# A searched order for the head of a fused attention and MLP kernel, with the fillers in free columns of a fixed PSUM bank

## The chip, the cores and the metric

The kernel runs on one core of a Trainium2 chip. The time is the device time of one execution in microseconds (us). The span in a profile is 1.7 to 1.8 us shorter than the time of the same execution (576.9 for 578.67 before).

PE is the matrix engine (TensorE), DVE is VectorE, ACT is ScalarE, POOL is GpSimd, SP is SyncE. The **head** is the work on batch 0 up to its MLP, some 45 us; the seven later batches run at full density behind it.

## The reference, cut to what matters

```python
# q, k, v: (8, 12, 448, 64); U (448, 32), V (32, 448); w_ch1 (768, 3072), w_ch2 (3072, 768)
q_n, k_n = rmsnorm(q, g_q), rmsnorm(k, g_k)      # x / sqrt(mean(x*x) + 1e-6) * g
attn = softmax(q_n @ k_n.T / 8)
x = (attn @ v)                                   # heads side by side: (8, 448, 768)
u = x + (x.T @ U @ V).T
out = u + relu(u @ w_ch1) @ w_ch2
```

## The kernel before

Inputs come in tiles of four heads of one batch; batch 0 has tiles 0, 1 and 2. For a tile, POOL or ACT squares q and k, DVE sums the squares (`reduce`), ACT makes the reciprocal root (`rsqrt`), DVE multiplies it in (`scale`), PE transposes (`turn`), and per pair of heads PE makes scores, ACT exponentials, PE weighs the values and DVE normalises. The head is a list of such pieces, and the schedule is by hand: each engine runs its instructions in the order of this list, and waits where an operand isn't ready (in the profile before, POOL stood 7.03 us for a scale of tile 2, with a cast and the issue of w1's third piece behind it in its order).

First, w1 is loaded in four pieces, and POOL issues them:

```python
def load_w1(i):
    c = (slice(0, 512), slice(512, 1024), slice(1024, 2048), slice(2048, 3072))[i]
    nc.gpsimd.dma_start(w1b[:, :, c], w1r[:, :, c])
```

The third piece, `load_w1(2)`, has hidden columns 1024 to 2047: blocks 8 to 15 of the first layer of the MLP need it. Second, a helper that makes POOL wait for a scale of DVE, by copying one element of its result. Third, the squares, which for tiles 2 to 5 are POOL's:

```python
def yield_port(t, pr):
    nc.gpsimd.tensor_copy(scratch, qkns[2 * t + pr][0:1, 1, 0, 0, 0:1])

def squares(t, hs=ALL, ss=(0, 1), eng=None):
    for s in ss:                                   # s = 0: k, s = 1: q
        ...
        if (t < 2 or t > 5) and eng is None:
            nc.scalar.activation(sqs[t, s][:, hs], qks[t, s][:, hs], AF.Square)
        else:
            nc.gpsimd.tensor_tensor(sqs[t, s][:, hs], qks[t, s][:, hs], qks[t, s][:, hs], OP.mult)
```

Fourth, the fillers, matmuls whose results nobody reads, and the list, here around `load_w1(2)`. The fillers are meant to keep PE's clock up:

```python
def heat(n):
    if n:
        warm = ps_mm.tile([P, 512], FP32, tag="mm")
        for _ in range(n):
            nc.tensor.matmul(warm, cold[:, 0:P], cold[:, 0:512], start=True, stop=True)

plan = [
    (heat, 16),
    ...
    (scores, 5, (0,)),
    (weigh, 3, 1),
    (load_w1, 2),
    (spread, 0),
    (squares, 3, ALL, (1,)),
    ...
]
```

## Time and profile before

| | before |
|---|---|
| time, median of 5 executions | 579.18 us (578.57 to 579.65) |
| span of the profiled execution | 576.9 us |
| PE busy | 560.0 us, 97% |
| MLP of batch 0 starts | 45.07 us |
| third piece of w1: issued, landed | 33.48, 50.25 us |
| block 8 starts (first use of that piece) | 50.29 us |

PE is busy nearly all the time, so the time goes with what PE loses, and it loses most in the head. The prediction below shows the page, the PE timeline and the chain of waits. The table of stretches before (stretch and its length, then busy time and count of PE, PE's weight loads, DVE, ACT and POOL, the granted PE clock, the DMA share and GB/s):

```profile
20.00:30.00 10.00, 8.40 (x101) 5.57 (x102) 7.90 (x19) 6.59 (x11) 4.66 (x8) 0.66 1.16 252
30.00:40.00 10.00, 10.00 (x177) 6.95 (x174) 8.49 (x24) 9.52 (x15) 7.62 (x7) 1.00 1.15 256
...
60.00:80.00 20.00, 18.34 (x194) 10.94 (x192) 16.78 (x40) 12.05 (x18) 7.36 (x10) 1.00 1.30 212
```

The clock was 0.66 in the mean from 20 to 30 us: the cold stretch. And the DVE timeline before, at the first scales of tile 2 (start, duration, engine, line, operation, tiles, count, and in brackets the idle time before and what ended it):

```profile
24.38 1.30 DVE L253 TENSOR_TENSOR qkn<-hT,rstd 112x512 bf16<-112x512 f32 x2 [0.19 <-issue]
```

Two scales in 1.30 us.

### The profile page before, as it was taken

Reading aid. Unit: us, or ns where it says so; the run is one execution under the profiler, and the core shown is the slowest. Engines: PE = TensorE matmul, PEld = TensorE weight load, DVE = VectorE, ACT = ScalarE, POOL = GpSimd, SP = SyncE. Lnnn points to the kernel's source line nnn. Section 1 sums busy time; section 2 is a strip of 40 time slices with the busy share of each in tenths; the row PEclk is TensorE's granted clock in tenths of the full one; section 3 lists DMA queues with packets and bytes.
Section 4 is the critical chain, followed back from the end, with each engine's and each line's share of the span. In section 5 each row is a group of like instructions: output and inputs, shape, how many; then the busy total and the mean of one; then the engine's idle time right before and its main releaser. Section 6 shows DMA issues by size and latency. Waiting matters only on the chain.

```text
span 576.9 us, 11306 instructions
## 1 busy us (share of the span) xinstructions
PE 560.0 (97%) x4607; PEld 306.5 (53%) x4607; DVE 387.1 (67%) x755; ACT 281.4 (49%) x419; POOL 79.0 (14%) x124
## 2 busy tenths in 40 slices
PE   5799999999999999999999999999999999999997
PEld 2465556544565555544465555644456555654464
DVE  4885964799875787647776598747767487453442
ACT  4777543376621875166641676246661475302200
POOL 4772510100020000000020000000011000000010
PEclk9799999999999999999999999999999999999999
DMA  9999985544443555544525455555334441050021
GB/s 212 243 252 226 216 139 141 129 118 88 112 136 93 117 135 126 114 99 113 129 75 116 105 130 120 125 132 128 82 79 127 122 97 33 28 110 1 1 55 55
DMA packets 103648, 67.22 MB, mean 117 GB/s; under 512 B 54716, under 2 KB 102060, under 8 KB 103596
## 3 DMA queue, kind: packets, MB, share of 16 engines
q1 hardware_dynamic: 93988, 56.77, 42.0%
q0 software_dynamic: 9376, 9.44, 9.8%
q8 instruction: 36, 0.59, 0.4%
q10 hardware_dynamic: 232, 0.30, 0.2%
q14 instruction: 16, 0.13, 0.1%
HBM read 52.19 MB, written 11.01 MB: 110 GB/s over the span
## 4 chain that ended last, share of the span: by engine, by line
PE 87%; DVE 4%; DMA 4%; ACT 1%; issue 0%; POOL 0%; DVEq 0%; ACTq 0%
PE ph L538 36%; PE pb L463 10%; PE po L463 8%; PE o L323 8%; PE pe L463 7%; PE pa L463 7%; PE sc L297 7%; DMA w1b<-in_moe_w_ch_dram 3%; DVE qkn L253 2%; PE pu L376 2%; ACT E L302 1%; DVE ring L378 1%; DMA u<-ring 1%; PE pm L362 1%; PE pt L264 0%
## 5 line engine op out<-in xcount | busy, mean ns | idle before, releaser
L538 PE MATMUL ph<-u,w1b 128*128 128x512 bf16 (+1 forms) x1128 | 232.6, 354 | 2.7 <-DVE qkT L275 1.2
L302 ACT ACTIVATE E<-sc 112x896 bf16<-112x896 f32 x184 | 159.8, 914 | 61.1 <-PE sc L297 61.0
L538 PEld LDWEIGHTS <-w1b 128*128 128x128 bf16 x1128 | 102.9, 98 | 110.9 <-issue 23.1
L463 PEld LDWEIGHTS <-hT 128*128 128x128 bf16 x1080 | 101.1, 98 | 71.1 <-issue 9.0
L541 ACT ACTIVATE hT<-ph 128x384 bf16<-128x384 f32 (+1 forms) x95 | 51.5, 542 | 130.7 <-PE ph L538 128.6
L543 DVE TENSOR_SCALAR hT<-ph 128x512 bf16<-128x512 f32 (+1 forms) x93 | 57.9, 622 | 57.0 <-PE ph L538 56.7
L323 PEld LDWEIGHTS <-E 112*128 112x128 bf16 x1472 | 59.8, 99 | 14.7 <-DVE ring L340 1.1
L323 PE MATMUL o<-va,E 112*128 112x65 bf16 x1440 | 62.1, 196 | 0.0
L253 DVE TENSOR_TENSOR qkn<-qk,rstd 112x512 bf16<-112x512 f32 x84 | 56.1, 707 | 7.2 <-ACT rstd L245 3.8
L297 PE MATMUL sc<-qkT 64*128 64x448 bf16 x384 | 55.9, 360 | 3.8 <-ACT E L302 2.2
L570 POOL COPY scratch<-qkn 1x1 bf16<-1x1 bf16 x44 | 11.1, 252 | 316.1 <-DVE qkn L253 316.1
L463 PE MATMUL po<-w2b,hT 128*128 128x384 bf16 x288 | 52.8, 326 | 0.1
L239 DVE TENSOR_REDUCE rstd<-sq 112x16 f32<-112x1024 f32 x40 | 48.4, 1211 | 4.7 <-ACT sq L231 4.7
L463 PE MATMUL pa<-w2b,hT 128*128 128x384 bf16 x264 | 49.5, 326 | 0.0
L463 PE MATMUL pb<-Tw,hT 128*128 128x384 bf16 x264 | 48.0, 326 | 0.0
L231 ACT ACTIVATE sq<-qk 112x1024 f32<-112x1024 f32 x36 | 38.2, 1061 | 8.1 <-DVE rstd L239 5.2
L378 DVE TENSOR_TENSOR ring<-pu,ring 128x768 bf16<-128x768 f32 (+3 forms) x36 | 31.0, 864 | 14.4 <-PE pu L376 13.8
L333 DVE RECIPROCAL rec<-o 128x4 f32<-128x4 f32 x96 | 17.1, 179 | 33.5 <-PE o L323 33.1
L340 DVE TENSOR_TENSOR ring<-o,rec 128x256 bf16<-128x256 f32 (+1 forms) x96 | 37.6, 391 | 2.4
L498 POOL TENSOR_TENSOR o<-o,ring 128x384 f32<-128x384 f32 x11 | 12.6, 1144 | 161.3 <-DVE o L497 161.3
L297 PEld LDWEIGHTS <-qkT 64*128 64x128 bf16 x384 | 12.7, 94 | 35.6 <-issue 32.0
L478 ACT ACTIVATE pb<-pa 128x384 f32<-128x384 f32 x11 | 5.2, 475 | 49.6 <-PE pa L463 49.6
(104 smaller groups left out, 424.1 us busy)
## 6 DMA issues: line engine op xcount, KB each, us to landing
qk<-in_k_dram SPq DMA_DIRECT2D x21, 448.0 KB, 5.4
vt<-in_v_dram SPq DMA_DIRECT2D x20, 448.0 KB, 4.7
qk<-in_q_dram SPq DMA_DIRECT2D x19, 448.0 KB, 3.8
w2b<-in_moe_w_ch_dram POOLq DMA_DIRECT2D x6, 768.0 KB, 14.8
w1b<-in_moe_w_ch_dram POOLq DMA_DIRECT2D x2, 1536.0 KB, 17.6
out_dram<-o SPq DMA_DIRECT2D x15, 168.0 KB, 2.3
out_dram<-o SPq DMA_DIRECT2D x16, 144.0 KB, 2.1
out_dram<-o SPq DMA_DIRECT2D x15, 120.0 KB, 2.1
```

Source lines behind the costliest of these rows:

```text
L231: nc.scalar.activation(sqs[t, s][:, hs], qks[t, s][:, hs], AF.Square)
L239: nc.vector.tensor_reduce(rstds[t][:, s, hs].rearrange("p h j -> p (h j)"), sqs[t, s][:, hs].rearrange("p h (j d) -> p (h j) d", d=D), AX, ...
L253: nc.vector.tensor_tensor(qkn[:, s].rearrange("p j h d -> p h j d"), qks[t, s][:, hp].rearrange("p h (j d) -> p h j d", d=D), rstd[:, s, h ...
L297: nc.tensor.matmul(sc[:, hh, 0:S], kT[pp, kc * SP:kc * SP + P], qT[pp, :], start=True, stop=True)
L302: nc.scalar.activation(E_of(p)[:, :, PAD + kc * S:PAD + (kc + 1) * S], scs.pop((p, kc))[0:SP, :, 0:S], AF.Exp, scale=float(D) ** 0.5)
L323: nc.tensor.matmul(o[:, n, :], E[:, hh, c:c + P], va[:, hl, kc, :], start=(kc == 0), stop=(kc == NJ - 1))
L340: nc.vector.tensor_tensor(ring[:, r0:r0 + t1 - t0, d0:d0 + D], o[:, t0:t1, 0:D], rec[:, t0:t1].rearrange("p c -> p c ()").to_broadcast([P, ...
L378: nc.vector.tensor_add(xv, pu[rows, 0:n, 0:HALF], xv)
L463: nc.tensor.matmul(ps, lhs[:, c, :], rhs[:, c, :], start=first and c == 0, stop=last and c == NC - 1, skip_group_check=again)
L538: nc.tensor.matmul(ph, w1b[:, dc, hc * P:(hc + 1) * P], u[:, dc, :], start=(dc == 0), stop=(dc == KD - 1))
L541: nc.scalar.activation(hT[:, hc, 0:n], ph, AF.Relu)
L543: nc.vector.tensor_relu(hT[:, hc, 0:n], ph)
```

## The change

The intent is to let PE lose less in the head. The order of the list was searched, with the fillers as pieces of their own (81 small ones in place of 29 large ones). The fillers no longer take a buffer from the rotating pool: they write to columns 272 to 511 of one fixed bank, whose first 260 columns hold the weighed values.

```diff
+    bank = ps_o.tile([P, 512], FP32, name="bank")
+    even = bank[:, 0:4 * (D + 1)].rearrange("p (i d) -> p i d", i=4)
+    warm = bank[:, 272:512]
...
-            o = ps_o.tile([P, 4, D + 1], FP32, tag="o")
+            o = even
...
-            (heat, 16),
+            (heat, 34),
             (grow2,),
+            (heat, 11),
... (most of the list moves; of these lines:)
+            (cast_u,),
             (expo, 0, 0),
...
             (load_w1, 0),
...
-            (gathered, 2),
+            (gathered, 2, 1),
+            (squares, 3, ALL, (1,)),
             (scores, 5, (0,)),
             (weigh, 3, 1),
             (load_w1, 2),
...
-            (squares, 3, ALL, (1,)),
...
-            warm = ps_mm.tile([P, 512], FP32, tag="mm")
             for _ in range(n):
-                nc.tensor.matmul(warm, cold[:, 0:P], cold[:, 0:512], start=True, stop=True)
+                nc.tensor.matmul(warm, cold[:, 0:P], cold[:, 0:240], start=True, stop=True)
```

The two lines about `squares(3, ALL, (1,))` put POOL's squaring of tile 3's q ahead of the issue of w1's third piece, so the issue must now wait for tile 3's q to arrive.

More of the change, by code (lines that the diff above doesn't have):

```diff
@@ L682, in head @@
             (reduce, 0, A, (1,)),
+            (rsqrt, 0, A),
             (reduce, 0, Bh, (0,)),
-            (rsqrt, 0, A),
             (squares, 0, Bh, (1,)),
-            (scale, 0, 0, (1,)),
             (reduce, 0, Bh, (1,)),
             (scale, 0, 0, (0,)),
+            (scale, 0, 0, (1,)),
             (rsqrt, 0, Bh),
+            (scale, 0, 1, (0,)),
             (scale, 0, 1, (1,)),
@@ L693, in head @@
             (gain,),
+            (heat, 3),
             (keep, 0, 0, 1),
+            (heat, 7),
             (yield_port, 0, 1),
@@ L697, in head @@
             (keep, 0, 1),
-            (scale, 0, 1, (0,)),
-            (heat, 4),
+            (squares, 2, ALL, (0,)),
             (scores, 0, (0,)),
+            (reduce, 1, ALL, (0,)),
             (turn, 1),
-            (squares, 2, ALL, (0,)),
-            (reduce, 1, ALL, (0,)),
+            (cast_u,),
             (expo, 0, 0),
             (scores, 0, (1,)),
+            (scores, 0, (2,)),
             (reduce, 1, ALL, (1,)),
@@ L708, in head @@
             (expo, 0, 1),
+            (keep, 1, 0),
             (rsqrt, 1),
-            (heat, 2),
-            (scores, 0, (2,)),
+            (heat, 13),
+            (keep, 1, 1),
+            (scale, 1, 0, (0,)),
+            (scale, 1, 0, (1,)),
+            (expo, 0, 2),
             (scores, 0, (3,)),
-            (keep, 1, 1),
-            (keep, 1, 0),
-            (scale, 1, 0, (1,)),
+            (scores, 1, (0,)),
             (squares, 2, ALL, (1,)),
-            (scale, 1, 0, (0,)),
@@ L718, in head @@
-            (expo, 0, 2),
-            (scale, 1, 1, (1,)),
-            (heat, 5),
-            (scores, 1, (0,)),
+            (expo, 0, 3),
+            (expo, 1, 0),
+            (scores, 1, (1,)),
+            (heat, 1),
             (turn, 2),
             (scale, 1, 1, (0,)),
-            (expo, 0, 3),
-            (cast_u,),
-            (expo, 1, 0),
-            (scores, 1, (1,)),
+            (scale, 1, 1, (1,)),
             (scores, 1, (2,)),
             (load, 4),
-            (heat, 2),
@@ L731, in head @@
-            (turn, 3),
-            (expo, 1, 1),
-            (scores, 1, (3,)),
-            (keep, 2, 0),
-            (expo, 1, 2),
-            (keep, 2, 1),
+            (keep, 2, 0),
+            (keep, 2, 1),
+            (expo, 1, 1),
+            (expo, 1, 2),
+            (cast_v, 0),
+            (setup_u, 0),
+            (heat, 5),
+            (reduce, 2, ALL, (0,)),
+            (scores, 1, (3,)),
+            (turn, 3),
             (expo, 1, 3),
             (scores, 2, (0,)),
-            (yield_port, 1, 0),
@@ L740, in head @@
-            (scores, 2, (1,)),
-            (cast_v, 0),
-            (expo, 2, 0),
-            (expo, 2, 1),
-            (reduce, 2, ALL, (0,)),
-            (reduce, 2, ALL, (1,)),
-            (setup_u, 0),
-            (scores, 2, (2,)),
-            (scores, 2, (3,)),
-            (keep, 3, 1),
-            (rsqrt, 2),
-            (setup_u, 1),
+            (scores, 2, (1,)),
+            (expo, 2, 0),
+            (heat, 7),
+            (expo, 2, 1),
+            (keep, 3, 0),
+            (scores, 2, (2,)),
@@ L752, in head @@
+            (weigh, 0, 0),
+            (reduce, 2, ALL, (1,)),
+            (setup_u, 1),
+            (rsqrt, 2),
+            (weigh, 0, 1),
+            (keep, 3, 1),
+            (load_v, 4),
+            (normalise, 0, 0),
+            (scores, 2, (3,)),
+            (yield_port, 1, 0),
+            (expo, 2, 2),
+            (scale, 2, 0, (0,)),
             (setup_u, 2),
             (cast_v, 1),
-            (load_v, 4),
-            (expo, 2, 2),
-            (keep, 3, 0),
-            (weigh, 0, 1),
@@ L758, in head @@
-            (scale, 2, 0, (0,)),
+            (expo, 2, 3),
             (yield_port, 1, 1),
-            (weigh, 0, 0),
-            (expo, 2, 3),
             (scores, 3, (0,)),
             (scale, 2, 0, (1,)),
-            (normalise, 0, 0),
+            (expo, 3, 0),
+            (turn, 4),
             (scores, 3, (1,)),
             (normalise, 0, 1),
-            (expo, 3, 0),
-            (turn, 4),
-            (weigh, 1, 0),
-            (setup_u, 3),
             (expo, 3, 1),
             (keep, 4, 0),
+            (keep, 4, 1),
@@ L773, in head @@
+            (setup_u, 3),
+            (scores, 3, (2,)),
+            (weigh, 1, 0),
+            (load, 5),
+            (weigh, 1, 1),
             (normalise, 1, 0),
-            (keep, 4, 1),
-            (load, 5),
-            (scores, 3, (2,)),
-            (weigh, 1, 1),
+            (load_w1, 1),
+            (gather, 0),
+            (expo, 3, 2),
             (scores, 3, (3,)),
-            (expo, 3, 2),
             (expo, 3, 3),
-            (weigh, 2, 0),
             (normalise, 1, 1),
@@ L783, in head @@
             (scores, 4, (0,)),
-            (gather, 0),
-            (expo, 4, 0),
-            (gather, 1),
+            (weigh, 2, 0),
             (scale, 2, 1, (0,)),
             (weigh, 2, 1),
-            (gathered, 1, 1),
+            (gather, 1),
             (gathered, 0, 1),
@@ L792, in head @@
             (load_v, 5),
+            (expo, 4, 0),
             (scores, 4, (2,)),
+            (gathered, 1, 1),
             (setup_v,),
@@ L796, in head @@
             (scale, 2, 1, (1,)),
-            (turn, 5),
-            (load_w1, 1),
             (normalise, 2, 0),
+            (cast_v, 2),
             (normalise, 2, 1),
             (expo, 4, 1),
+            (yield_port, 2, 1),
             (weigh, 3, 0),
-            (yield_port, 2, 1),
-            (spreaded, 1),
-            (gather, 2),
+            (turn, 5),
             (scores, 4, (3,)),
@@ L808, in head @@
             (keep, 5, 0),
-            (expo, 4, 3),
-            (cast_v, 2),
             (keep, 5, 1),
+            (gather, 2),
+            (spreaded, 1),
             (normalise, 3, 0),
-            (gathered, 2),
+            (gathered, 2, 1),
+            (squares, 3, ALL, (1,)),
             (scores, 5, (0,)),
@@ L816, in head @@
             (load_w1, 2),
+            (expo, 4, 3),
+            (expo, 5, 0),
+            (weigh, 4, 1),
+            (normalise, 4, 1),
+            (weigh, 4, 0),
+            (scores, 5, (1,)),
             (spread, 0),
-            (squares, 3, ALL, (1,)),
-            (weigh, 4, 1),
-            (scores, 5, (1,)),
             (normalise, 3, 1),
-            (expo, 5, 0),
+            (spread, 2),
+            (normalise, 4, 0),
+            (expo, 5, 1),
             (spreaded, 0, 1),
+            (gather, 3),
             (scores, 5, (2,)),
-            (weigh, 4, 0),
-            (normalise, 4, 1),
-            (expo, 5, 1),
-            (gather, 3),
-            (spread, 2),
             (squares, 3, ALL, (0,)),
-            (normalise, 4, 0),
-            (gathered, 3, 1),
-            (scores, 5, (3,)),
+            (gathered, 3),
             (spread, 3),
             (spreaded, 2),
+            (scores, 5, (3,)),
             (reduce, 3),
@@ L838, in head @@
             (expo, 5, 2),
+            (spreaded, 3, 1),
+            (first, 0, (0, 1, 2), True),
             (squares, 4, ALL, (0,)),
             (cast_v, 3),
-            (first, 0, (0, 1, 2), True),
             (expo, 5, 3),
             (weigh, 5, 1),
-            (spreaded, 3, 1),
             (weigh, 5, 0),
@@ L857, in head @@
             (spread, 5),
+            (first, 1, (4,), False),
+            (spreaded, 5, 1),
             (first, 0, (4,), False),
-            (spreaded, 5, 1),
-            (first, 1, (4,), False),
-            (first, 0, (5,), False),
             (first, 1, (5,), False),
@@ L864, in head @@
             (load_w1, 3),
+            (first, 0, (5,), False),
         ]
```

## The prediction

> **What bounds the kernel now.** I read the page first, then the chain of waits over the first 60 us, then the timelines of PE, ACT, DVE and POOL up to 80 us, and last the DMA view in short stretches. The page, with the span in 40 slices of 14.4 us:
> ```profile
> span 576.9 us, 11306 instructions
> ...
> PE   5799999999999999999999999999999999999997
> ...
> PEclk9799999999999999999999999999999999999999
> DMA  9999985544443555544525455555334441050021
> ```
> PE is busy in nine tenths or more of every slice but the first two and the last, so the end is set by PE: what the change can win is time that PE loses in the first slices (to 29 us). Two other things are wrong just there: the clock row has its one 7 in the second slice, and the DMA row is full for five slices. The PE timeline (start, duration, engine, line, operation, tiles, count):
> ```profile
> 24.68 1.94 PE L323 MATMUL o<-va,E 112*128 112x65 bf16 x32
> 26.55 0.93 PE L297 MATMUL sc<-qkT 64*128 64x448 bf16 x4
> ...
> 36.50 0.55 PE L297 MATMUL sc<-qkT 64*128 64x448 bf16 x4
> ...
> 45.07 3.09 PE L538 MATMUL ph<-u,w1b 128*128 128x384 bf16 x18
> ...
> 50.29 1.15 PE L538 MATMUL ph<-u,w1b 128*128 128x384 bf16 x6 [0.27 <-DMA w1b<-in_moe_w_ch_dram]
> ```
> The part that the change rewrites ends at 45.07, where the MLP of batch 0 starts. Four score matmuls take 0.93 us at 26.55 and 0.55 us at 36.50: PE ran slow around 24.7 to 29.2 (the table of stretches gives a clock of 0.50 there). But the last line is the important one. At 50.29, five microseconds into the MLP, PE waits for a piece of w1 (the third of four, hidden columns 1024 to 2047, needed from block 8 on). The wait is only 0.27 us, and the chain of waits shows why it matters:
> ```profile
> 33.48 16.77 DMA w1b<-in_moe_w_ch_dram
> 50.24 0.05 issue
> 50.29 1.16 PE ph L538 x6
> ```
> The transfer was issued at 33.48 and landed at 50.25. PE arrives at 50.02 without it. So the head and this transfer finish in a dead heat: a faster head alone wins 0.27 us, and then waits.
>
> What decides the landing? POOL's timeline around the issue, and the DMA view of the stretch 36 to 38 us (queue: packets, MB, share; q0 carries what POOL issues, q1 what SP issues):
> ```profile
> 32.37 0.18 POOL L570 COPY scratch<-qkn 1x1 bf16<-1x1 bf16 x1 [7.03 <-DVE qkn L253]
> 32.49 1.03 POOL L221 CAST Tw<-hT 112x1024 bf16<-112x1024 f32 x1
> 33.48 0.83 POOL L181 DMA_DIRECT2D w1b<-in_moe_w_ch_dram  x1
> ```
> ```profile
> q1 hardware_dynamic: 508, 0.50, 108.4%
> q0 software_dynamic: 3, 0.00, 0.6%
> ```
> POOL stood idle 7.03 us for the scale of tile 2, and issued the third piece late. The second piece (issued 24.45) landed at 36.7, and for the 2 us after that POOL's queue moved nothing: from an issue to its first packets go some 4.5 to 6 us (33.48 to about 38; the first piece, 16.12 to about 22). Then the third piece needs 12 us (1.57 MB; the stretch 38 to 50 moved 1.84 MB on q0 while q1 shared the engines). All the while the engines are full: 199 to 300 GB/s in every 1.5 us from 3 us up to 60 us.
>
> [...] the first sixteen fillers start every 0.43 us and from 6.05 on every 0.21, and the score matmuls above differ by a factor of 1.7. [...] (q1 108% in the stretch where q0 had 0.6%, 30.5% in 38 to 50 where q0 had 80.8%). [...]
> ```profile
> 17.25 2.38 DVE L253 TENSOR_TENSOR qkn<-Tw,rstd 112x512 bf16<-112x512 f32 x1
> ```
> where the same scale otherwise takes 0.68 to 0.70 us; POOL squared tile 2 from 17.16 to 19.08.
>
> **The change part by part.** The comparison of instruction orders shows the same 222 DMA issues on SP in the same order; on the compute engines the order differs in the head only (the last 8553 PE rows agree apart from waits).
>
> Fillers: 29 of 512 columns become 81 of 240 (45 before the first transpose, then 10, 13, 1, 5, 7). [...] one of 240 is about 0.10 us, so 45 take 14 cold (0.2 each) plus 31 warm, 6.0 us, and end near 9.2, before the transposes at about 10.2. The later ones sit where PE waits for ACT's exponentials: 13 are 1.3 us[...]. They cost nothing on the path if they end before the next exponential has freed its scores, which by hand they just do. [...] the cold stretch (weigh 1.94 against 1.35, scores 0.93 against 0.55, transposes 0.93 against 0.57, weigh 1.09 against 0.68) costs 1.7 us before, 0 after.
>
> Order: both scales of tile 1's second pair now come straight after the first pair's, at about 17.0 to 18.2, while the second squaring on POOL moves to about 18.7 (behind cast_u and the first w1 issue). [...] lets the transposes of pair 3 start at about 19.5 instead of 20.38. ACT, which before sits idle 1.25, 1.25 and 0.88 us for scores between 21 and 30, then runs nearly without gaps. Walking on by the durations of before, the MLP starts at 42 to 43.5 instead of 45.07: **2 to 3 us earlier**. Its first four blocks, the transposes and scores between them take 4.95 us (45.07 to 50.02), so PE reaches block 8 at about 47 to 48.5.
>
> Transfers: load_w1(0) goes behind cast_u, which waits for U; U was issued after tile 2's q (landed 16.7), so the issue goes from 16.12 to about 17.7. First packets at 23.7 instead of 22.2; pieces one and two take 13.4 us of q0 at the old rate, to 37.1. Piece three is issued behind the scale of tile 2 (now about 29.5), tile 3's q (landed 30.4) and one squaring of 1.9 us: about 32.2, so 1.3 us earlier; plus 4.7 us it is ready at 36.9, so the hole in q0 closes. Start 37.1, 12 us of packets, 0.3 us to the semaphore: **landing 49.4**, 0.85 us earlier than before.
>
> Static bank: pool rotation gone. In the later batches each weigh on this bank loses a PE wait on itself, and the weights' wait for DVE becomes the matmul's. The page gives 0.0 us idle before these matmuls, so I count 0.
>
> Sum: block 8 at 49.4 or 49.5 instead of 50.29, minus 0.8 to 0.9 us; everything behind it is PE at full density in an unchanged order. The stalls at 52.13 (0.74, for an exponential queued behind block 8's relu) and 62.15 (0.95, a scale of 2.4 us beside POOL's squaring) hang on PE's own progress and stay. 579.25 - 0.9 = **578.3 us**.
>
> **The rivals.** (1) The head counts in full: 2 to 3 us, 576.5 or so. For it: that is what the order was searched for. Against it: the 0.27 us wait; it needs the w1 piece to land at 47, which full engines do not give. (2) The transfer comes later: U lands late, piece one slips by more than the closed hole returns, and the landing is at 50.3 or later: 579.3 to 580. For it: load_w1(0) behind a cast with a DMA wait, and a squaring before load_w1(2). (3) PE waits so long at block 8 that its clock falls[...]. (4) The removed PE self-waits pay in all seven later batches[...]. Against it: no idle is recorded there.
>
> **Range and chances.** The landing is uncertain by about 1 us each way, rival 4 pulls down, rivals 2 and 3 up: 576.7 to 579.8. Two per cent is 11.6 us, and all of PE's idle time is 17 us, of which 9 are in the head: faster 0.01, same 0.98, slower 0.01.
>
> **What would show it.** Right: the clock row loses its 7; the MLP starts at 42 to 44; no scale over 1 us before 25 us; q0 without a hole; a wait of 1 to 2.5 us on w1b at about 49.4, the longest of PE in the first 60 us. Wrong: the piece landing before 48.5 or after 50.3, no w1b wait at all (the head was not faster), or a stretch after 60 us that differs from before by more than 0.5 us.

Where the text is cut, it said something of the hardware that no trace here shows. The sum stands as it was put on record: 579.25 - 0.9 = 578.3 us, range 576.7 to 579.8. Its 0.9 us is the landing at 49.4 instead of 50.29, and no part of that is cut. (Its 0.3 us to the semaphore is about what the trace before shows for the second piece: last packet done at 36.31, landing at 36.7.) Cut are terms of the head's 2 to 3 us and of the rivals: a rate for warm fillers (in the trace before, those of 512 columns start every 0.43 us and later every 0.21, so by estimate 0.20 and 0.10 for 240 columns), a length for one exponential (two in a row start 0.80 us apart there), the assumption that the fillers hold the clock, on which the "0 after" of the cold stretch rests, the reason why the moved squaring was to save 1.7 us (the scale of 2.38 us beside POOL's squaring less the usual 0.68), and what rivals 3 and 4 would cost or pay.

## The result, and the profile after

The median was **581.94 us** (580.56 to 582.21, 5 executions) against 579.18 us of the kernel before in the same rounds. Ratios here are the mean time of one kernel's fast runs over the mean of the other's of the same rounds, so not quite the ratio of the medians quoted. The ratio is 1.0043, 95% interval 1.0027 to 1.0058: within 2%, but slower, and outside the predicted range of 576.7 to 579.8.

The page after, as the page before in the prediction (span in 40 slices of 14.5 us):

```profile
span 580.4 us, 11396 instructions
...
PE   7699999999999999999999999999999999999997
...
PEclk9989999999999999999999999999999999999999
DMA  8999994545543556547434465475234641040021
```

The low digit of the clock row became 8 and moved one slice on. The table of stretches says it more sharply:

```profile
20.00:30.00 10.00, 6.27 (x77) 3.74 (x77) 9.84 (x17) 5.44 (x9) 6.28 (x9) 0.88 1.15 246
30.00:40.00 10.00, 9.62 (x169) 7.02 (x168) 6.46 (x20) 7.47 (x11) 4.87 (x5) 0.78 1.13 251
...
60.00:80.00 20.00, 18.34 (x195) 10.80 (x193) 18.06 (x40) 11.50 (x18) 10.27 (x12) 1.00 1.28 206
```

From 20 to 40 us the clock before lost 10 x (1 - 0.66) = 3.4 us of full speed, and after 10 x (0.12 + 0.22) = 3.4 us. The cold stretch was moved, not removed. On top of it PE was busy 2.1 us less from 20 to 30 us. From 60 to 80 us PE is busy 18.34 us in both. Most of the loss lies in the head: the span is 3.5 us longer, and block 8 starts 2.98 us later. The other 0.5 us is what two much later waits leave. At 234 us PE waits for DVE and did not before:

```profile
234.40 0.67 PE L326 MATMUL bank<-va,E 112*128 112x65 bf16 x16 [1.42 <-DVE ring L343]
```

DVE had itself waited 3.26 us there for a transfer (1.85 before). A wait of 0.8 to 1.6 us at this place, 228 to 235 us, is in all nine profiles below that have the changed order or a version of it, order_only without the fixed bank included, and in none of the five with the old order. Those have a wait of 0.7 to 0.9 us for a transfer at 514 to 520 us instead. So the head's order also shifts what happens in later batches; why, no run here shows.

The PE timeline after:

```profile
27.51 0.53 PE L267 MATMUL pt<-ident,qkn 112*128 112x112 bf16 x4 [1.72 <-DVE qkn L256]
28.88 0.55 PE L267 MATMUL pt<-ident,qkn 112*128 112x112 bf16 x4 [0.84 <-DVE qkn L256]
...
48.39 3.09 PE L541 MATMUL ph<-u,w1b 128*128 128x384 bf16 x18
...
53.27 0.99 PE L541 MATMUL ph<-u,w1b 128*128 128x384 bf16 x5
```

The MLP starts at 48.39, which is 3.32 us later than before; block 8 starts at 53.27 with no wait for w1 (before: 50.29). PE waits 1.72 and 0.84 us for scales of tile 2. The DVE timeline after shows those scales and an earlier one, of tile 1:

```profile
17.16 2.98 DVE L256 TENSOR_TENSOR qkn<-qk,rstd 112x512 bf16<-112x512 f32 x1
...
25.07 3.75 DVE L256 TENSOR_TENSOR qkn<-hT,rstd 112x512 bf16<-112x512 f32 x2
```

One scale takes 2.98 us where an undisturbed one takes 0.68, and the two of tile 2 take 3.75 us where they took 1.30 before. What POOL did at those times, and when it issued the pieces of w1, is on its timeline after:

```profile
16.65 1.01 POOL L184 DMA_DIRECT2D w1b<-in_moe_w_ch_dram  x1
17.68 1.91 POOL L236 TENSOR_TENSOR w2b<-hT 112x1024 f32<-112x1024 f32 x1
...
24.83 1.04 POOL L224 CAST va<-Tw 112x1024 bf16<-112x1024 f32 x1 [1.19 <-DMA Tw<-in_v_dram]
...
34.11 0.18 POOL L573 COPY scratch<-qkn 1x1 bf16<-1x1 bf16 x1 [4.03 <-DVE qkn L256]
34.26 1.88 POOL L236 TENSOR_TENSOR w2b<-hT 112x1024 f32<-112x1024 f32 x1
36.10 0.89 POOL L184 DMA_DIRECT2D w1b<-in_moe_w_ch_dram  x1
```

The squaring of tile 2 runs from 17.68 to 19.59, in the middle of the long scale of 17.16 to 20.14; the cast of v1 at 24.83 lies beside the next. And the third piece of w1 is issued at 36.10, not 33.48. It landed 16.4 us later, at 52.5 (before: 50.25).

So two causes lay open, and in this profile they end almost together: the head was slow by itself (block 8 reached at 53.27), and w1's third piece came late (52.5). PE came 0.8 us after the piece and did not wait for it. My theory at this point was the first, scales that run long beside POOL's work (2.98 us for one, 3.75 for two) and slow the head, with the late piece as a floor under it. The rivals were the late issue as the main term, and the bank.

### The profile page after: what moved, and what is told of

It is laid out like the page before. It is cut to its first block, busy times and chain, and to the rows that moved or that the text cites. A ratio compares the mean times of both kernels' runs of the same rounds, so it can differ in the third digit from the quotient of the medians.

```text
span 580.4 us, 11396 instructions
## 1 busy us (share of the span) xinstructions
PE 562.7 (97%) x4659; PEld 312.3 (54%) x4659; DVE 390.7 (67%) x755; ACT 281.9 (49%) x419; POOL 79.3 (14%) x124
## 4 chain that ended last, share of the span: by engine, by line
PE 90%; DVE 4%; DMA 2%; ACT 1%; issue 1%; SPq 0%; DVEq 0%; ACTq 0%
PE ph L541 37%; PE pb L466 11%; PE po L466 8%; PE pe L466 7%; PE pa L466 7%; PE sc L300 7%; PE bank L326 7%; DVE qkn L256 2%; PE pu L379 2%; DMA Tw<-in_q_dram 2%; PE o L326 1%; ACT E L305 1%; DMA qkT<-qkn 1%; PE first L885 1%; DVE rstd L242 1%
## 5 line engine op out<-in xcount | busy, mean ns | idle before, releaser
L326 PEld LDWEIGHTS <-E 112*128 112x128 bf16 x1472 | 59.4, 99 | 16.4 <-issue 3.5
L256 DVE TENSOR_TENSOR qkn<-qk,rstd 112x512 bf16<-112x512 f32 x84 | 58.5, 738 | 7.3 <-ACT rstd L248 4.0
L326 PE MATMUL bank<-va,E 112*128 112x65 bf16 x1280 | 54.5, 194 | 1.8 <-DVE ring L343 1.4
L242 DVE TENSOR_REDUCE rstd<-sq 112x16 f32<-112x1024 f32 x40 | 48.4, 1211 | 5.0 <-ACT sq L234 4.8
L343 DVE TENSOR_TENSOR ring<-bank,rec 128x192 bf16<-128x192 f32 (+1 forms) x83 | 32.3, 389 | 1.9
L336 DVE RECIPROCAL rec<-bank 128x4 f32<-128x4 f32 x83 | 14.8, 178 | 27.3 <-PE bank L326 26.9
L300 PEld LDWEIGHTS <-qkT 64*128 64x128 bf16 x384 | 12.3, 94 | 34.6 <-issue 30.5
## 6 DMA issues: line engine op xcount, KB each, us to landing
w1b<-in_moe_w_ch_dram POOLq DMA_DIRECT2D x2, 1536.0 KB, 17.7
```

The costliest lines, as they stand in the source:

```text
L242: nc.vector.tensor_reduce(rstds[t][:, s, hs].rearrange("p h j -> p (h j)"), sqs[t, s][:, hs].rearrange("p h (j d) -> p (h j) d", d=D), AX, ...
L256: nc.vector.tensor_tensor(qkn[:, s].rearrange("p j h d -> p h j d"), qks[t, s][:, hp].rearrange("p h (j d) -> p h j d", d=D), rstd[:, s, h ...
L300: nc.tensor.matmul(sc[:, hh, 0:S], kT[pp, kc * SP:kc * SP + P], qT[pp, :], start=True, stop=True)
L326: nc.tensor.matmul(o[:, n, :], E[:, hh, c:c + P], va[:, hl, kc, :], start=(kc == 0), stop=(kc == NJ - 1))
L343: nc.vector.tensor_tensor(ring[:, r0:r0 + t1 - t0, d0:d0 + D], o[:, t0:t1, 0:D], rec[:, t0:t1].rearrange("p c -> p c ()").to_broadcast([P, ...
```

## The experiments

Twelve runs were made of eight kernels, in three calls. Runs of one call share a chip and the runs of the kernel before: 579.15 us in call 1, 579.65 in call 2, 580.8 in call 3 (medians of 11). The chips differed, so compare within a call.

### Call 1: the kernel again, its two parts alone, and the scales kept apart from POOL

**again** is the changed kernel, unedited, for a second profile.

> The changed kernel once more, unedited, beside the kernel before on one chip. If the loss belongs to the program: ratio 1.003 to 1.006, the MLP of batch 0 starts near 48.4 us (45.07 before), two scales of tile 2 take over 3 us together at about 25 us. If the one profile caught an unlucky arrival of v (landing 22.5 and 24.8 us): ratio under 1.002 and the scales of tile 2 at 1.3 us.

Measured: 582.84 us (578.9 to 583.92), ratio 1.0040 [1.0010, 1.0069]. The PE timeline of this run, and the chain of waits up to block 8 (start, duration, what):

```profile
45.76 3.09 PE L541 MATMUL ph<-u,w1b 128*128 128x384 bf16 x18
...
53.00 1.58 PE L541 MATMUL ph<-u,w1b 128*128 128x384 bf16 x6 [2.30 <-DMA w1b<-in_moe_w_ch_dram]
```
```profile
15.63 19.05 DMA hT<-in_q_dram
34.68 0.07 issue
34.75 1.84 POOL w2b L236
36.59 16.36 DMA w1b<-in_moe_w_ch_dram
52.96 0.05 issue
```

The ratio is the expected one, but the profile is not: the MLP was expected near 48.4 and the two scales of tile 2 at over 3 us, and they came at 45.76 and 2.23 us. Here the head came out 2.6 us faster than in the first profile (MLP at 45.76), and nothing was won: PE waited 2.30 us for w1. The chain has no PE in it at all before 53.00. It runs from tile 3's q (landed 34.68), through one squaring, to the issue at 36.59 and the landing. Block 8 itself then took 1.58 us instead of 1.15: after the wait the granted clock was lower (0.83 in the mean from 50 to 60 us, 1.00 in the first profile).

**bank_only** has the order of before and the fixed bank, each filler of 512 columns as two of 240.

```diff
... (the bank and its two parts as in the change)
-            warm = ps_mm.tile([P, 512], FP32, tag="mm")
-            for _ in range(n):
-                nc.tensor.matmul(warm, cold[:, 0:P], cold[:, 0:512], start=True, stop=True)
+            for _ in range(2 * n):
+                nc.tensor.matmul(warm, cold[:, 0:P], cold[:, 0:240], start=True, stop=True)
```

> Order of before, but the fixed bank for o and fillers (each 512-column filler as two of 240). If the bank costs or pays in all later batches (77 weighs): a ratio off 1 by 0.2% or more, with the difference growing after 100 us. If the order is the cause: ratio 0.999 to 1.001, and the MLP starts at 44.8 to 45.4 us.

Measured: 580.51 us (579.13 to 581.43), ratio 1.0010 [0.9991, 1.0029]. No effect can be told from nothing, though up to 0.3% (1.7 us) is not excluded. The MLP started at 46.20, later than the 44.8 to 45.4 expected.

**order_only** has the order and the filler counts of after, but takes buffers for the fillers and the weighed values from the rotating pools as before.

```diff
... (the bank and its two parts go)
-            o = even
+            o = ps_o.tile([P, 4, D + 1], FP32, tag="o")
...
+            warm = ps_mm.tile([P, 512], FP32, tag="mm")
             for _ in range(n):
-                nc.tensor.matmul(warm, cold[:, 0:P], cold[:, 0:240], start=True, stop=True)
+                nc.tensor.matmul(warm[:, 0:240], cold[:, 0:P], cold[:, 0:240], start=True, stop=True)
```

> Order and filler counts of the changed kernel, but o and fillers in the rotating buffers as before. Order theory: as slow as the changed kernel, ratio 1.003 to 1.006, MLP start 47.5 to 49. Bank theory: ratio 1.000.

Measured: 582.11 us (580.15 to 583.04), ratio 1.0040 [1.0017, 1.0062], the same as the whole change in the same call. The loss is the order's; a smaller effect of the bank beside it is not excluded.

**ports_apart** is the changed kernel with POOL's second squaring of tile 2 put behind the scales of tile 1, its cast of v1 behind those of tile 2, and w1's second piece issued earlier.

```diff
-            (squares, 2, ALL, (1,)),
...
             (scale, 1, 1, (1,)),
+            (yield_port, 1, 1),
+            (squares, 2, ALL, (1,)),
...
             (cast_v, 0),
+            (load_w1, 1),
...
-            (yield_port, 1, 0),
-            (cast_v, 1),
-            (yield_port, 1, 1),
...
             (scale, 2, 0, (1,)),
+            (yield_port, 2, 0),
+            (cast_v, 1),
...
-            (load_w1, 1),
```

Behind the expectation stands the first theory: a scale runs long beside POOL's work, as in the first profile (2.98 us at 17.16, and 3.75 for two at 25.07).

> The changed kernel with POOL kept off DVE's scales: the second squaring of tile 2 waits for the last scale of tile 1, and the cast of v1 waits for the first two scales of tile 2 (the second piece of w1 is issued before it). [...] every scale before 35 us under 1.2 us, the clock holds, the MLP starts 3 to 5 us earlier than in the changed kernel (43.5 to 45.5), and the time falls to 578.3 to 579.5 because the third piece of w1 lands near 50. Rival (late transfers of q, k, v set the head): scales fast, but the MLP still starts after 47 us and the ratio stays over 1.003.

Measured: 583.5 us (582.08 to 585.18), ratio 1.0066 [1.0042, 1.0090]: slower still, where 578.3 to 579.5 was expected. The edit did what it was made for. The four scales of tile 1 took 0.80, 0.77, 0.68 and 0.68 us, the first two of tile 2 together 1.28, the clock was 1.00 from 20 to 30 us, and PE reached the first early blocks of the MLP at 36.59 instead of 42.31. Then all of it was given back. One line each of its DVE and its PE timeline, and its chain of waits:

```profile
39.19 2.35 DVE L242 TENSOR_REDUCE rstd<-w2b 112x16 f32<-112x1024 f32 x2 [3.16 <-POOL w2b L236]
```
```profile
42.69 0.24 PE L401 MATMUL pm<-ring,Ub 128*32 128x128 bf16 x4 [2.50 <-DVE ring L343]
...
53.25 1.15 PE L541 MATMUL ph<-u,w1b 128*128 128x384 bf16 x6 [1.47 <-DMA w1b<-in_moe_w_ch_dram]
```
```profile
14.35 20.08 DMA hT<-in_q_dram
34.43 0.07 issue
34.51 1.84 POOL w2b L236
36.35 16.85 DMA w1b<-in_moe_w_ch_dram
```

DVE stood 3.16 us at the sums of tile 3, whose squares wait for the same q; the normalising of the last pair is behind them in DVE's order, and PE waited 2.50 us for it; PE ran slow behind that wait (eight matmuls of the first early blocks took 2.61 us at 44.39, 1.46 at 38.72), and the MLP started at 46.83 (43.5 to 45.5 expected). And at block 8 there was the same chain as in **again**, link by link. My theory that the scales beside POOL were the main term did not stand by itself here: taking them away did not make the kernel faster. What both runs have in common is that tile 3's q, which nothing in the head of batch 0 needs, sits ahead of things that it does need.

### Call 2: the place of the third issue, forward and backward

**before_w1_late** does only one thing of the change, to the kernel before.

```diff
             (weigh, 3, 1),
+            (squares, 3, ALL, (1,)),
             (load_w1, 2),
             (spread, 0),
-            (squares, 3, ALL, (1,)),
```

> The kernel before with one swap: tile 3's squaring of q (which waits for q to arrive) stands ahead of the issue of w1's third piece on POOL, as the change has it. If that place is the cause: issue at 34 to 36.5 us instead of 33.5, landing 16.5 us later at 50.5 to 53, PE waits for it 0.5 to 3 us at block 8, ratio 1.001 to 1.005. If only the order of the compute engines matters: ratio 1.000 and the wait stays at 0.3 us.

Measured: 580.87 us (580.24 to 581.94), ratio 1.0021 [0.9996, 1.0046]. POOL and PE timelines of this run:

```profile
34.22 1.88 POOL L233 TENSOR_TENSOR w2b<-hT 112x1024 f32<-112x1024 f32 x1
36.05 0.89 POOL L181 DMA_DIRECT2D w1b<-in_moe_w_ch_dram  x1
```
```profile
52.74 1.15 PE L538 MATMUL ph<-u,w1b 128*128 128x384 bf16 x6 [2.01 <-DMA w1b<-in_moe_w_ch_dram]
```

Moving one line made a wait of 2.01 us where the kernel before has one of 0.27, with block 8 at 52.74. The mechanism is plain in the profile; the time moved in the expected direction, but the interval just touches 1.

**w1_early** undoes only this, in the changed kernel: the third piece goes right behind the second.

```diff
             (load_w1, 1),
+            (load_w1, 2),
...
-            (load_w1, 2),
```

> The changed kernel with only the issue of w1's third piece moved up, right behind that of the second. If its late issue sets the end: landing at 49 to 51 instead of 52.5 to 53, no wait at block 8, time 580 to 581 (the head still starts its MLP at 45.8 to 48.4), ratio 1.001 to 1.003. If scales beside POOL alone set it: as the changed kernel, 1.004.

Measured: 578.61 us (577.98 to 581.21), ratio 0.9992 [0.9966, 1.0018]. The slowdown is gone, and by more than the expected 1.001 to 1.003. PE timeline:

```profile
47.14 3.09 PE L541 MATMUL ph<-u,w1b 128*128 128x384 bf16 x18
...
52.02 1.15 PE L541 MATMUL ph<-u,w1b 128*128 128x384 bf16 x6
```

There is no wait for w1 (landed at 49.6, issued at 27.9). The profiled execution was the slowest of the six (581.21), and its head still carries a scale of 2.98 us, so what is left of the loss in this profile is the head's own.

**before_w1_early** does the same to the kernel before.

```diff
             (load_w1, 1),
+            (load_w1, 2),
...
-            (load_w1, 2),
```

> The kernel before with only the issue of w1's third piece moved up, right behind the second. The dead heat of the prediction: the 0.27 us wait at block 8 goes, nothing else changes, ratio 0.998 to 1.000; landing 48 to 49.5.

Measured: 580.38 us (578.26 to 581.66), ratio 1.0014 [0.9988, 1.0040]. A miss: the wait did not go. PE timeline:

```profile
51.58 1.15 PE L538 MATMUL ph<-u,w1b 128*128 128x384 bf16 x6 [0.69 <-DMA w1b<-in_moe_w_ch_dram]
```

The piece was issued 5 us earlier (28.48) and landed at 51.5, no earlier than before: 23.1 us from issue to landing. It is no clean test: in this profile the second piece itself went out at 27.59 (24.45 before), with the third right behind it. In time no gain can be told.

**unblocked** is ports_apart with the third piece right behind the second, and with DVE's sums and scales of tile 3 moved behind the work of batch 0.

```diff
             (load_w1, 1),
+            (load_w1, 2),
...
-            (reduce, 3),
...
-            (rsqrt, 3),
             (normalise, 5, 1),
             (normalise, 5, 0),
+            (reduce, 3),
             (gather, 5),
-            (scale, 3, 0),
...
             (first, 1, (5,), False),
+            (rsqrt, 3),
+            (scale, 3, 0),
             (scale, 3, 1),
```

> The version with POOL kept off the scales, and in addition w1's third piece issued right behind the second and tile 3's sums, roots and scales put behind the last normalisation, so that the arrival of tile 3's q holds up neither. If these two places are where the gain of that version was lost (a wait of 2.50 us for the normalisation and 1.47 us for w1): both waits under 0.5 us, MLP start 43.5 to 44.5, ratio 0.994 to 0.998, faster than both kernels. Rival, the full transfer engines: w1's third piece lands at 50.5 or later all the same and the ratio is 1.000 or more.

Measured: 579.42 us (576.34 to 582.65), ratio 0.9998 [0.9962, 1.0034], where 0.994 to 0.998 was expected. The six executions fall into two groups: 576.34, 577.54 and 577.96, and 580.88, 580.91 and 582.65. The profile is the fastest of them, the fastest execution of any kernel here:

```profile
42.42 3.09 PE L541 MATMUL ph<-u,w1b 128*128 128x384 bf16 x18
...
47.67 1.15 PE L541 MATMUL ph<-u,w1b 128*128 128x384 bf16 x6 [0.24 <-DMA w1b<-in_moe_w_ch_dram]
```

The head of the prediction (MLP at 42 to 43.5, block 8 at 47 to 48.5) does exist, with the long scales beside POOL and both waits for tile 3 out of its way; that it is missing in the slower executions fits their times and the one profile of them below.

### Call 3: the closest cases once more, on another chip

These have no new edit.

> The changed kernel unedited, on one chip with its repaired version, because the two were measured in different calls so far. All theories: ratio 1.003 to 1.005; w1's third piece issued at 36 to 36.6 us and landing 16.4 to 16.9 us later.

Measured (changed kernel): 581.32 us (580.34 to 582.52), ratio 1.0012 [0.9990, 1.0034]: below the 1.003 to 1.005 expected, so on this chip the slowdown itself is not clear of the noise. The profile repeats the first one: a scale of 2.98 us at 17.30, two of tile 2 in 3.97, MLP at 48.54, block 8 at 53.45.

> The changed kernel with only the third w1 issue moved up, second sample. If the late issue is the main term: 2 us or more under the changed kernel of the same call, no w1 wait at block 8 in the profile. If the earlier ratio of 0.9992 was the luck of that chip: under 1 us away from it.

Measured: 579.89 us (577.88 to 581.12), ratio 0.9984 [0.9957, 1.0011]. Again no wait for w1; block 8 at 51.89. By the means this is 1.65 us under the changed kernel, short of the 2 us expected, and the two ranges overlap.

> The kernel before with only the swap of tile 3's squaring and the third w1 issue, second sample. Main-term theory: 1 to 2.5 us over the kernel before, landing 52 to 53, a w1 wait of 1 us or more. Otherwise 1.000.

Measured: 581.5 us (578.87 to 583.51), ratio 1.0003 [0.9977, 1.0029]. The profile has the wait again, 2.57 us (third piece issued at 36.83, landed at 54.0), and the clock 0.77 from 50 to 60 us. In time this is a miss: 1 to 2.5 us over the kernel before was expected, and no difference can be told.

> The version that keeps POOL off the scales and takes tile 3's arrival out of the way, second sample. Its first runs lay at 576.3 to 578.0 and at 580.9 to 582.7. If the early profile of this run shows v1 at 22 and tile 3's q at 31 us: near 576.5. If it shows 24 and 34: over 580, with the loss before 40 us. That would make the arrival of q, k and v the second term, apart from the order.

Measured: 578.58 us (576.57 to 582.07), ratio 0.9977 [0.9946, 1.0008]. This time the profile is one of the slow executions (582.07): tile 3's q landed at 35.6, v1 at 24.7, and the scales of tile 3 now come so late that PE waits for them behind the MLP's start:

```profile
45.71 3.09 PE L541 MATMUL ph<-u,w1b 128*128 128x384 bf16 x18
...
50.58 0.37 PE L267 MATMUL pt<-ident,qkn 112*128 112x112 bf16 x4 [1.07 <-DVE qkn L256]
```

### All profiles side by side

| profile | tile 3's q landed | MLP starts | third piece issued | landed | block 8 starts | rest of the span |
|---|---|---|---|---|---|---|
| before | 30.4 | 45.07 | 33.48 | 50.25 | 50.29 | 526.6 |
| after | 34.1 | 48.39 | 36.10 | 52.5 | 53.27 | 527.1 |
| again | 34.7 | 45.76 | 36.59 | 53.0 | 53.00 | 528.4 |
| again_2 | 34.9 | 48.54 | 36.79 | 53.4 | 53.45 | 527.3 |
| order_only | 33.7 | 47.77 | 35.67 | 52.1 | 52.64 | 527.0 |
| ports_apart | 34.4 | 46.83 | 36.35 | 53.2 | 53.25 | 527.1 |
| before_w1_late | 30.3 | 45.79 | 36.05 | 52.7 | 52.74 | 527.5 |
| before_w1_late_2 | 30.9 | 46.56 | 36.83 | 54.0 | 54.07 | 527.6 |
| bank_only | 32.3 | 46.20 | 34.60 | 51.2 | 51.20 | 527.3 |
| w1_early | 34.9 | 47.14 | 27.9 | 49.6 | 52.02 | 527.4 |
| w1_early_2 | 32.1 | 47.01 | 24.9 | 48.1 | 51.89 | 527.3 |
| before_w1_early | 32.2 | 45.95 | 28.5 | 51.5 | 51.58 | 526.6 |
| unblocked | 30.8 | 42.42 | 22.1 | 47.6 | 47.67 | 526.9 |
| unblocked_2 | 35.6 | 45.71 | 24.3 | 47.5 | 52.93 | 527.4 |

Read the last two columns first. The rest of the span behind block 8 is 526.6 to 527.6 us whatever was changed, and 528.4 in **again** (in **again** and in both profiles of before_w1_late the clock had cooled at block 8: 0.83, 0.83 and 0.77 from 50 to 60 us). So the start of block 8 tells most of the span, to within about 1 us, and block 8 starts at the later of two things: PE's arrival, about 5 us behind the MLP's start (7.2 in unblocked_2, which waits for scales of tile 3), and the landing. Where the third piece was issued between 33.5 and 36.8 us it landed 16.4 to 17.2 us later, so the landing follows the issue almost one for one. In the nine profiles that have this piece at its place of before or of after, the issue came at 33.5 and 34.6 us where it is ahead of tile 3's squaring, and at 35.7 to 36.8 in the seven where it is behind. What the issue then waits for last is not always the same: q in **again** and ports_apart, by 2.5 us and more; q and the scale within 0.3 us of each other in after, again_2 and order_only; and in before_w1_late the second scale of tile 2, with the squaring of 1.88 us as the extra time.

Over all three calls and the first rounds, the changed kernel has a mean of 581.66 us (17 executions), w1_early 579.34 (12), the kernel before 579.91 (38), unblocked 579.32 (12). Calls and chips are mixed in these means; within call 3 alone, w1_early is 1.65 us below the changed kernel (means of six each).

**What stays open.** Transfers of q, k and v come in early or late. Tile 3's q landed at 30.3 to 32.3 us in the five profiles that have the order of before, and at 30.8 to 35.6 in the nine that have the changed order, although SP issues the same 222 transfers in the same order in both. SP issued it at 14.23 before and 15.43 after, and from there to its landing it took 16.2 and 18.7 us. So the changed order mostly sees it later, but not always: unblocked, one kernel, had it at 30.8 in one profile and at 35.6 in another, on another chip. This goes with the two groups of unblocked, whose two profiles are an execution of the fast group and one of the slow; what makes the transfers late, and whether the order has a part in it, no run here shows. No version was found that is clearly faster than the kernel before: unblocked has the lowest mean and the fastest execution, and its intervals contain 1.

## Why the prediction was wrong

**The bound was right as a bound.** The prediction said that the head and the landing of w1's third piece end in a dead heat, and that a faster head alone wins nothing. **again** shows just that (a wait of 2.30 us for w1 with the MLP at 45.76). But both ends of the dead heat came later, not earlier. Rival 2, the transfer comes later, is what happened to the landing, by the second of its two reasons, "a squaring before load_w1(2)"; the first did not come, since U and the first piece were earlier than reckoned (issue 16.65, not 17.7). And all three signs of being wrong came true: a landing after 50.3 (52.5), no wait for w1 in the first profile, and a stretch after 60 us that differs by more than 0.5 us (the 1.42 us at 234 us).

**Two steps failed, one at each end.** The first, at the transfer, is this one: "Piece three is issued behind the scale of tile 2 (now about 29.5), tile 3's q (landed 30.4) and one squaring of 1.9 us: about 32.2, so 1.3 us earlier". The rule in it was right and both numbers that it uses were not. The 30.4 for q was read from the profile of before and treated as a fixed time; in the changed kernel's three profiles q landed at 34.1, 34.7 and 34.9. In the order of before the issue did not depend on q at all, so its arrival was free to vary; the change put it on the path. The scale was late too, because the head was: POOL was released by it at 34.11, 32.04 and 34.58 instead of 29.5. In the first profile the two came together, and the same rule gives 34.11 + 0.15 + 1.88 = 36.1, which is the 36.10 of the issue. In **again** POOL had the scale at 32.04 and then waited 2.53 us for q alone.

**The closed hole in q0 did not come**, but that only follows from the late issue: q0 had 4.9% of the engines' time from 38 to 39 us. The transfer itself was reckoned well. The prediction gave it 17.2 us from issue to landing (32.2 to 49.4), and it took 16.4 (16.8 before). So the landing at 52.5 instead of 49.4 is the issue's 3.9 us less 0.8.

**The second failed step, at the head, is the 1.7 us that the moved squaring was to save** (the scale of 2.38 us less 0.68). The squaring was expected at 18.7, with U landing at about 17 and its cast taking 0.74 us. U landed at 16.3, the cast took 0.31, so the squaring came at 17.68, and the scale at 17.16 took 2.98 us instead of the 2.38 before. "No scale over 1 us before 25 us" was wrong already at 15.42 (1.13 us), and the scales of tile 2, undisturbed before, took 3.75 us for two. The clock did not hold either: the cold stretch was to vanish, and as much clock was lost as before, 3.4 us of full speed from 20 to 40 us. So the MLP started at 48.39 and not at 42 to 43.5. ports_apart shows that scales with POOL's squaring behind them take 0.68 to 0.80 us.

**How the two failures share the loss.** In the profiled execution either alone would have cost about the same: the head reached block 8 at 53.27, the piece landed at 52.5. Taking away the first only (ports_apart) left the time slow. Taking away the second only (w1_early) brought it back to that of before, in both calls. So by the times the late issue is the larger term. That is in part argued. In three of the four profiles that have the changed order as it is and the late issue (after, again_2 and order_only; the fourth is **again**) PE reached block 8 0.1 to 0.8 us behind the landing and did not wait, so there a removed wait can't be the gain; in the other direction, before_w1_late made the wait each time (2.01 and 2.57 us) but no time clear of the noise; and w1_early also moves a transfer of 1536 KB among those that the head waits for. The head's slowness has a part that this does not separate, since a late scale of tile 2 also delays the issue. w1_early's profiles also have the MLP 1.3 to 1.4 us earlier than the first profile of the changed kernel; I can't tell whether that is the edit or the arrivals.

**What held.** No effect of the bank can be told (1.0010, interval containing 1). The stalls at blocks behind 8 stayed: 0.74 for the exponential and 0.96 for the scale, where 0.74 and 0.95 were expected. Rival 3 is there too: with waits for w1 of 2.3 us (**again**) and 2.6 us (before_w1_late_2, in the old order) the clock was 0.83 and 0.77 from 50 to 60 us.

## What to carry to other kernels

Before moving a DMA issue in an in-order engine queue, look at what stands in front of it: if that waits for another transfer, the issue inherits that transfer's arrival (in **again** q landed at 34.68 and the issue came at 36.59, one squaring later), and here one moved squaring made the issue some 2 us later, enough to hide a head that was 2.6 us faster in one execution than in another. A landing time read from one profile is not a constant, so take it from several executions before building on it, and ask what the old order did not depend on. When one delay is removed and the time does not move, follow the chain of waits again before giving up the theory: two delays that end within 1 us of each other, as here at 52.5 and 53.27, have to be removed together. And look behind the part that was changed: here 0.5 us of 3.5 came from a wait at 234 us.

## What the runs show of the hardware, and what they leave open

- In the first profile of the changed kernel a scale started at 17.16 and POOL's squaring at 17.68; the squaring took its usual 1.91 us and the scale 2.98 instead of 0.68. w1_early and w1_early_2 show another 2.98 each, with a squaring that began 0.52 us behind the scale, as here. A DMA issue stood on POOL when each of these scales began (16.65 to 17.66 in the first). In unblocked two scales beside the same issue (16.89 to 17.91), with no squaring right behind it, took 0.77 and 0.68 us; but the scale that began at 25.07 in the first profile, beside the cast of v1, ended at 27.45, 0.62 us behind the end of the second piece's issue and not of the cast (25.87). What makes a scale long, the squaring, the issue or both, the runs do not separate.
- Single waits of 2.01 to 2.57 us at block 8 went with a mean clock of 0.83 to 0.77 over the 10 us from 50 to 60 (**again** and both profiles of before_w1_late). After one of 1.47 us in ports_apart block 8 took 1.15 us, no more than without a wait. In the first profile of the changed kernel, waits of 1.72 and 0.84 us in a stretch with PE busy 6.27 of 10 us went with 0.88 from 20 to 30 us and 0.78 from 30 to 40. From what length on a wait lowers the clock is not shown.
- The third piece, 1536 KB, took 16.4 to 17.2 us from issue to landing where it was issued at its place of before or of after, and 21.7 to 25.5 us when issued right behind another piece, with a DMA share of 1.11 to 1.17 in every table of stretches taken from 20 to 50 us. That set the landing here.
- The arrival of a transfer differed by 4.8 us between two executions of one kernel on two chips (unblocked: tile 3's q at 30.8 and 35.6 us).
